# Last attention layer of a four-layer transformer kernel: values as narrow weights, block transposes at a group's end, GpSimd for some shifted copies

## The chip, the cores and the metric

The kernel runs on one core of one Trainium2 chip. Its engines run side by side, each with its own queue of instructions in a fixed order: PE (TensorE, matrix multiplies), DVE (VectorE), ACT (ScalarE), POOL (GpSimd) and SP (SyncE, which issues DMAs). PE writes into PSUM, eight banks of 512 float32 columns by 128 partitions; the others read from there and from SBUF. The metric is the device time of one execution in microseconds (us); the median over runs is compared.

## The reference

An activation `x` of 2048 tokens by 512 channels goes through four layers, each `x = x + f(layernorm(x))`: A, B, A, B. Both have 32 heads of 16 channels.

Layer A cuts the tokens into four segments of 512. Inside a segment it is causal softmax attention; beside it stands a linear-attention memory `M`, `z` that is summed over the earlier segments, and a gate per head mixes the two. Layer B is plain attention over all 2048 tokens:

```
scores = einsum('bhqd,bhkd->bhqk', q, k) * Dh ** (-0.5)
p = softmax(scores)
o = einsum('bhqk,bhkd->bhqd', p, v)
x = x + o.reshape(B, S, D) @ wo
```

All tensors are bfloat16. Nothing subtracts a row maximum in the kernel: it takes exponentials, sums them with a column of ones beside the values, and divides at the end.

## The kernel before, in words

**A planner writes the program.** The class `Sched` (lines 69 to 190) records every operation with its dependencies, and keeps an estimate of the time at which each engine would have done it. `Builder` walks through the work unit by unit, and decides from these estimates what goes next and to which engine. The result is a fixed order of instructions for each engine with semaphore waits between them; on the chip nothing is decided any more.

**Groups and tiles.** Work is cut into groups (`Group`, line 224): one layer, one segment of 512 queries, and four heads (one in each 32-partition quarter `r`). A group of layer B with all four key segments has 64 tiles, a tile being 128 keys by 512 queries of one head. `make_groups` (line 1108) lists them. Layers 0 to 3 overlap in time, since a later layer's segment 0 starts while the earlier layer's last segments run; only the last layer's query segments 1 to 3, 24 groups of 64 tiles, stand alone at the end. Query segment 0 of layers B is done in waves over the key segments, with partial sums kept in SBUF.

**A unit** (`unit`, line 1191) takes two or three tiles for ACT. Their score matmuls (tile `qm,KB`, 32 rows of the array each, four quarters of the rows beside one another) go to banks 0 to 2 or 4 to 6 in turn, ACT takes the exponential of all of them in one instruction (line 1244) into `pT`, and in layers A POOL masks the diagonal blocks (line 1259). Two units later the value products follow.

**Tiles on DVE.** Some tiles of layers B have their exponential made on DVE instead: `dx_find` and `dx_take` (lines 826, 838) take up to a third of a group's tiles, and `compose` (line 1265) puts them beside a unit's tiles. `dx_first` (line 891; the operation is at line 900) reads one or two score banks and turns them with one multiply and add into 16-bit integers whose bits are a bfloat16 near the exponential. `dx_chain` (line 928; line 946) makes three more images of a pair, each by adding a constant. The four images' errors cancel for the most part, so such a tile costs four value products where a tile of ACT costs one. A pair needs four slots of 128x1024 16-bit: nine in `dxw`, and six more in `KA`, `QA`, `VA` once layer 0 no longer needs their second halves (`dx_space`, `dx_widen`, lines 852 and 870). `dx_room` (line 820) lets DVE fall behind by no more than `DQ` = 2200 ns of the estimate. `dx_chain` could give a copy to POOL, but `POOL_ON` is 0.

**The value product** (`pv`, line 1286). The exponentials, 128 keys by 128 queries, are the weights, and the 17 columns of a head's values and ones stream through. A 512-query tile takes four such pairs of weight load and matmul, and its results stand by query in bank 7 (`ACC`), 16 blocks of 17 columns. Products of ACT's tiles are due two units after; products of DVE's images are fitted in by `pv_taken` (line 1364), up to four in a unit, and all that are left when the group ends (`pv_step`, line 1379).

**A group's end** (`finish`, line 1312): a reciprocal of the sums (line 1333) and a product (line 1345) give `ob`, by query. After the second of two groups `run_deferred` (line 1351) sends `ob` through a DMA transpose to `oT`, channels by queries, for the output projection (`task_out`, line 736). The very last group goes through two pairs of PE transposes instead (`last_out`, line 779).

**Beside that** projections, layer norms and output projections are tasks that fill in where the estimates leave room (`bg_one`, line 1013), and `keep_busy` (line 375) issues dummy matmuls (`wB,zero`) where PE's streams would fall under 43% of a window. All recorded matmuls have line 389, or 393 for transposes.

## Time and profile before

| | us |
|---|---|
| three runs | 1953.49, 1959.38, 1965.37 |
| median | 1959.38 |
| the profiled execution | 1956.4 |
| its span, first to last instruction | 1954.7 |
| ACT busy | 1828.6 |
| PE busy | 1761.4 |
| DVE busy | 1500.5 |
| POOL busy | 285.0 |

A row of the groups names line, engine, operation, output and inputs (buffer numbers left out), shapes and count; then busy time in us and the mean of one in ns; then the idle time of the engine just ahead of them, and who ended it. A row of the stretches gives start and end, length, and each engine's busy time with the number of instructions that started, then PE's granted clock as a share, the DMA share and GB/s. A row of the timeline has start, length, engine, line, operation and count; neighbours of one kind are merged into one row. PE is the matmuls, PEld the weight loads.

### The profile page before, as it was taken

Reading aid. Unit: us, or ns where it says so; the run is one execution under the profiler, and the core shown is the slowest. Engines: PE = TensorE matmul, PEld = TensorE weight load, DVE = VectorE, ACT = ScalarE, POOL = GpSimd, SP = SyncE. Lnnn points to the kernel's source line nnn. Section 1 sums busy time; section 2 is a strip of 40 time slices with the busy share of each in tenths; the row PEclk is TensorE's granted clock in tenths of the full one; section 3 lists DMA queues with packets and bytes.
Section 4 is the critical chain, followed back from the end, with each engine's and each line's share of the span. In section 5 each row is a group of like instructions: output and inputs, shape, how many; then the busy total and the mean of one; then the engine's idle time right before and its main releaser. Section 6 shows DMA issues by size and latency. Waiting matters only on the chain.

```text
span 1954.7 us, 79981 instructions
## 1 busy us (share of the span) xinstructions
PE 1761.4 (90%) x35997; PEld 1135.1 (58%) x36232; DVE 1500.5 (77%) x3154; ACT 1828.6 (94%) x1641; POOL 285.0 (15%) x642
## 2 busy tenths in 40 slices
PE   7788888889979999899997999889899999999998
PEld 4344444556646666466664666445666666666665
DVE  5656566788858887688876888577888888888886
ACT  6789988899999999899998999988999999999998
POOL 3432153010050000500005000320100000000000
PEclk9999999999999999899999999999999999999999
DMA  4110111000011000100001001000000000000000
GB/s 152 27 36 18 29 21 31 14 11 11 10 27 16 3 8 14 34 9 14 8 14 37 5 6 24 18 8 13 11 16 9 6 17 6 6 6 16 6 6 16
DMA packets 101016, 35.96 MB, mean 18 GB/s; under 512 B 93505, under 2 KB 100161, under 8 KB 100673
## 3 DMA queue, kind: packets, MB, share of 16 engines
q1 hardware_dynamic: 100672, 30.83, 8.1%
q8 instruction: 283, 4.64, 1.0%
q14 instruction: 61, 0.49, 0.1%
HBM read 6.30 MB, written 2.10 MB: 4 GB/s over the span
## 4 chain that ended last, share of the span: by engine, by line
PE 37%; ACT 36%; DVE 12%; issue 12%; DMA 2%; POOL 1%; SPq 0%; ACTq 0%; DVEq 0%; POOLq 0%
PE ps L389 37%; ACT pT L1244 36%; DVE dxw L900 2%; DVE dxw L946 1%; DMA xT<-xn 1%; DVE ob L1345 1%; POOL pT L1259 1%; ACT amem L584 1%; DVE VA L900 0%; DVE QA L900 0%; DVE rd L1333 0%; DVE QA L946 0%; DVE KA L946 0%; DVE VA L946 0%; DVE KB L416 0%
## 5 line engine op out<-in xcount | busy, mean ns | idle before, releaser
L1244 ACT ACTIVATE pT<-ps 128x1536 bf16<-128x1536 f32 (+3 forms) x1600 | 1799.6, 1260 | 100.6 <-PE ps L389 80.4
L389 PEld LDWEIGHTS ps<-VB,pT 128*128 128x128 bf16 x12872 | 427.9, 96 | 324.6 <-issue 233.3
L389 PE MATMUL ps<-qm,KB 32*128 32x512 bf16 x4096 | 524.4, 387 | 63.2 <-ACT pT L1244 45.8
L389 PE MATMUL ps<-VB,pT 128*128 128x51 bf16 (+1 forms) x12872 | 551.7, 187 | 28.9 <-DVE ob L1345 16.4
L900 DVE TENSOR_SCALAR dxw<-ps 128x512 uint16<-128x512 f32 (+1 forms) x365 | 333.4, 915 | 85.3 <-PE ps L389 80.9
L389 PE MATMUL ps<-VB,dxw 128*128 128x51 bf16 (+1 forms) x8520 | 362.1, 186 | 0.9 <-DVE dxw L946 0.9
L1259 POOL TENSOR_SCALAR_AFFINE_SELECT pT<-pT 128x256 bf16<-128x256 bf16 (+2 forms) x513 | 209.6, 427 | 552.6 <-ACT pT L1244 543.3
L389 PEld LDWEIGHTS ps<-VB,dxw 128*128 128x128 bf16 x8520 | 282.3, 96 | 1.4 <-DVE dxw L946 1.1
L389 PEld LDWEIGHTS ps<-qm,KB 32*128 32x128 bf16 x4096 | 130.0, 91 | 179.0 <-ACT pT L1244 97.7
L1161 POOL TENSOR_SCALAR qm<-QB,par 128x512 bf16<-128x512 bf16 x86 | 68.1, 794 | 1020.2 <-PE ps L389 895.1
L946 DVE TENSOR_SCALAR dxw<-dxw 128x1024 uint16<-128x1024 uint16 (+1 forms) x454 | 182.8, 423 | 3.3 <-PE ps L389 0.7
L389 PE MATMUL ps<-qm,KA 32*128 32x512 bf16 (+3 forms) x1024 | 105.0, 312 | 36.0 <-ACT pT L1244 31.4
L389 PE MATMUL ps<-VA,pT 128*128 128x51 bf16 (+1 forms) x2560 | 114.9, 190 | 22.8 <-DVE ob L1345 14.4
L389 PEld LDWEIGHTS ps<-VA,pT 128*128 128x128 bf16 x2560 | 87.1, 98 | 79.1 <-POOL pT L1259 43.5
L389 PEld LDWEIGHTS ps<-qm,KA 32*128 32x128 bf16 x1024 | 30.0, 92 | 112.5 <-ACT pT L1244 77.8
L900 DVE TENSOR_SCALAR KA<-ps 128x512 uint16<-128x512 f32 (+1 forms) x91 | 80.2, 882 | 18.8 <-PE ps L389 17.6
L389 PE MATMUL ps<-VB,QA 128*128 128x51 bf16 (+1 forms) x1848 | 90.0, 186 | 0.0
L900 DVE TENSOR_SCALAR VA<-ps 128x512 uint16<-128x512 f32 (+1 forms) x83 | 75.2, 906 | 18.7 <-PE ps L389 17.6
L389 PE MATMUL ps<-VB,KA 128*128 128x51 bf16 (+1 forms) x1844 | 89.0, 185 | 0.1
L389 PE MATMUL ps<-VB,VA 128*128 128x51 bf16 (+1 forms) x1836 | 87.3, 185 | 0.0
L900 DVE TENSOR_SCALAR QA<-ps 128x512 uint16<-128x512 f32 (+1 forms) x82 | 74.5, 909 | 14.5 <-PE ps L389 13.8
L1333 DVE RECIPROCAL rd<-ps 128x16 f32<-128x16 f32 x112 | 28.3, 253 | 69.6 <-PE ps L389 69.1
(125 smaller groups left out, 1540.0 us busy)
## 6 DMA issues: line engine op xcount, KB each, us to landing
out_dram<-x SPq DMA_DIRECT2D x8, 256.0 KB, 2.2
x<-in_A_x_dram SPq DMA_DIRECT2D x3, 512.0 KB, 9.0
wB<-in_B_wqkv_dram SPq DMA_DIRECT2D x1, 1536.0 KB, 13.0
oT<-ob SPq DMA_TRANSPOSE x63, 2.4
xT<-xn SPq DMA_TRANSPOSE x60, 2.5
x<-in_A_x_dram SPq DMA_DIRECT2D x4, 128.0 KB, 2.2
wA<-in_A_wk_dram SPq DMA_DIRECT2D x1, 512.0 KB, 4.7
wA<-in_A_wq_dram SPq DMA_DIRECT2D x1, 512.0 KB, 5.7
```

The source lines that it names most:

```text
L389: self.sc.add("pe", lambda e: e.matmul(out, lhsT, rhs, start=start, stop=stop, skip_group_check=True), reads=reads, banks=[(bank, "w", all ...
L584: self.op("act", lambda e: e.activation(et, src, ACT.Exp), reads=bsrc, writes=self.b_amem, ns=1023, gap=915)
L900: self.sc.add("dve", lambda e: e.tensor_scalar(d, o, SCALE * LOG2E * 128, EXP_C, op0=ALU.mult, op1=ALU.add), writes=[w for j in range(k) f ...
L946: self.op(eng, (lambda o, d: lambda e: e.tensor_scalar(o, w, d, None, op0=ALU.add))(o, d), reads=bw, writes=wr, ns=ns, name="dxs")
L1161: self.op(eng, (lambda m, q, col: lambda e: e.tensor_scalar(m, q, col, 0.0, op0=ALU.mult, op1=ALU.add))(m, q, col), reads=[bq, self.b_par] ...
L1244: self.sc.add("act", (lambda dst, src: lambda e: e.activation(dst, src, ACT.Exp, scale=SCALE))(dst, src), writes=self.b_pT[slot * 3 + i:sl ...
L1259: self.op("pool", (lambda blk, pat: lambda e: e.affine_select(blk, blk, pattern=pat, compare_op=ALU.is_ge, fill=0.0, base=0, channel_multi ...
L1333: self.op("dve", lambda e: e.reciprocal(rd, src[:, :, 16]), reads=bsrc, writes=[br], bank=bk, alloc=al, ns=253)
L1345: self.op("dve", lambda e: e.tensor_tensor(ob, src[:, :, 0:16], rb, ALU.mult), reads=[br] + bsrc, writes=[self.b_ob[oi][g.e]], bank=bk, al ...
```

## The change

Six things, most of them for the last layer's groups of 64 tiles (`g.fm`):

1. `pv`: for these groups the 17 columns of values and ones are the weights, and the 512 queries of a tile stream through in one matmul. Its tile of the array is all 128 rows by 32 columns; head `r` uses column quarter `r` and PSUM partitions `32r` to `32r + 16`. The result stands by channel in bank 7, 512 columns.
2. `finish_fm`: at a group's end DVE transposes the bank in 32x32 blocks into `tk` (float32, in the dead half of `KA`), takes the reciprocal of column 16 of each block, multiplies into `of` by query, and after the second group of a pair `run_deferred` transposes `of` in blocks into `oT`. The DMA transposes of these groups go. The last group does this in two halves, in place of the PE transposes.
3. `pv_some` takes the place of `pv_taken`: products due now and shifted products are put in an order in which the column quarter that is free soonest comes first. `pv_close` lets a group's last shifted products wait for a later step, where they were forced at once.
4. POOL may make a shifted copy: `POOL_ON` goes from 0 to 300 and its assumed cost `POOL_T` from 1150 to 1800, so a copy goes to POOL where by the estimate it would be done at most 300 ns after DVE gets there. This holds in layer 1 too, once the first slots have opened. `DQ` goes from 2200 to 3000.
5. `dx_areas`: up to 38 slots in memory that is no longer used (`QA`, `VA`, `wA`, `KA`, `woA`, `phk`, `phq`, keys and values of key slots 2 and 3, `xT`), each opened when the flags that it needs are set, in place of six.
6. The planner's estimate knows column tiles: 30 ns from one to the next, and half a full pass's weight in the activity that `keep_busy` watches.

The two programs in instructions: PE 36232 matmuls before, 28291 after; DVE 3154 and 2811; POOL 638 and 1142; ACT 1640 and 1638; SP 194 and 183.

```diff
             st = max(ready, self.pe_issue())
+            if cols < 128:
+                st = max(st, self.pe_issue() + 30)
...
-            self.streams.append((st, n / 2.4 * rows / 128))
+            self.streams.append((st, n / 2.4 * rows / 128 * max(cols / 128, self.CW)))
...
+        self.fm = kind == "B" and Builder.FM >= (1 if L == 3 and first and last else 2 if L == 3 else 3 if first and last else 4)
...
-    DX_T, POOL_T, POOL_ON = 430, 1150, 0
+    DX_T, POOL_T, POOL_ON = 430, 1800, 300
...
-    DQ, DXS, PVN, PVLATE, PVWAIT = 2200, 4, 4, 600, 0
+    DQ, DXS, PVN, PVLATE, PVWAIT, PVHOLE = 3000, 4, 4, 600, 0, 100
...
+    def dx_areas(self):
...
+        first = (("attn", 0, 3), ("mem", 0, 3))
+        add(flat(self.QA[:, 1, :, :]), 2, lambda j: self.b_QA[1], *first)
+        add(flat(self.VA[:, 1, :, :]), 2, lambda j: self.b_VA[1], *first)
+        add(flat(self.wA[:, :, :]), 6, lambda j: self.b_wA, ("proj", 2, 3))
+        last = (("attn", 2, 3), ("mem", 2, 3), ("op", 2, 3))
+        add(flat(self.KA[:, 0, :, :]), 2, lambda j: self.b_KA[0], *last)
...
+        for ks in (2, 3):
+            add(flat(self.KB[:, ks, :, :]), 2, lambda j: self.b_KB[ks], ("attn", 3, 0))
+            add(flat(self.VB[:, ks, :, :]), 2, lambda j: self.b_VB[ks], ("attn", 3, 0))
+        for k in range(2):
+            add(flat(self.xT[:, k, :, :]), 2, lambda j: self.b_xT[k], ("in", 3, 3))
...
     def dx_widen(self):
 
-        if not self.wide and ("attn", 0, 3) in self.flags and ("mem", 0, 3) in self.flags:
-            self.wide = True
-            self.dx_bufs += range(self.NDX, self.NDX + 6)
+        for n, (_, _, need) in enumerate(self.areas[:self.XDX]):
+            if n not in self.dx_open and all(f in self.flags for f in need):
+                self.dx_open.add(n)
+                self.dx_bufs.append(self.NDX + n)
+                self.wide = True
...
+        if g.fm:
+            g.left -= 1
+            self.mm(self.ps[32 * r:32 * r + 17, bank.col0:bank.col0 + 512], parts[0][2], pT[:, 0:512], r not in g.started, g.left == 0,
+                    [bp, parts[0][3]], bank, g.acc, tile=(128, 0, 32, 32 * r))
+            g.started.add(r)
+            parts = ()
...
+    def finish_fm(self, g, src, bsrc, bk, al):
...
+        for j in range(halves):
+            sl = slice(512 // halves * j, 512 // halves * (j + 1))
+            tk, rd = self.tk[:, sl], self.rd[:, m, n * j:n * j + n]
+            self.op("dve", (lambda tk, a: lambda e: e.transpose(tk, a))(tk, src[:, sl]), reads=bsrc, writes=[self.b_tk] + extra, bank=bk,
+                    alloc=al, ns=690 if halves == 1 else 420)
+            t3 = tk.rearrange("p (n f) -> p n f", f=32)
+            self.op("dve", (lambda rd, t3: lambda e: e.reciprocal(rd, t3[:, :, 16]))(rd, t3), reads=[self.b_tk], writes=[self.b_rd[m]], ns=160)
...
+            self.op("dve", (lambda of, t3, rb: lambda e: e.tensor_tensor(of, t3[:, :, 0:16], rb, ALU.mult))(of, t3, rb),
+                    reads=[self.b_rd[m], self.b_tk], writes=[self.b_of[g.e]], ns=430 if halves == 1 else 300)
...
+            if g.fm:
+                o = self.oT[:, 1, g.c, :]
+                op = self.op("dve", (lambda o: lambda e: e.transpose(o, self.of))(o), reads=self.b_of, writes=[self.b_oT[1][g.c]], ns=690)
...
+    def pv_some(self, g, due, now):
...
+        while True:
+            cand = [(self.pv_quad(e[3]), 0, n) for n, e in enumerate(due)]
+            for n, t in enumerate(self.dxq):
+                if t[1] is g and (now or t[0].end + LAG[t[0].eng] <= self.sc.t["pe"] + self.PVWAIT):
+                    cand.append((self.pv_quad(t[3]), 1, n))
+            if not cand:
+                return
+            q, kind, n = min(cand)
...
+            if not due and not now and q + self.PVHOLE > max(self.pv_quad(r) for r in range(4)) and (
+                    used >= self.PVN or self.sc.t["pe"] > self.sc.t["act"] - self.PVLATE):
+                return
...
+    def pv_close(self, g, must):
...
+        if not whole():
+            self.pv_some(g, (), must)
...
+            if not whole():
+                return 0
+        self.cur = self.pend = None
+        cost = self.finish(g)
```

## The prediction

> **What bounds the kernel now.** I read the page's top first, then the busy time by stretches, cut where the last stretch is the one that the change touches most: from 1421 us on only the last layer's 24 groups of 64 tiles are left (query segments 1 to 3).
>
> ```profile
> span 1954.7 us, 79981 instructions
> PE 1761.4 (90%) x35997; PEld 1135.1 (58%) x36232; DVE 1500.5 (77%) x3154; ACT 1828.6 (94%) x1641; POOL 285.0 (15%) x642
> ```
> ```profile
> core 0: us, PE busy (x) PEld busy (x) DVE busy (x) ACT busy (x) POOL busy (x), PEclk, DMA share, GB/s
> 0.00:442.00 442.00, 371.42 (x5728) 207.22 (x5795) 288.56 (x692) 381.92 (x359) 128.31 (x309) 0.97 0.17 37
> 442.00:1167.00 725.00, 660.81 (x13710) 433.95 (x13804) 574.35 (x1251) 686.89 (x626) 96.72 (x218) 0.98 0.08 14
> 1167.00:1421.00 254.00, 225.22 (x4368) 138.86 (x4406) 188.96 (x407) 235.61 (x209) 44.94 (x95) 0.99 0.08 15
> 1421.00:1949.00 528.00, 502.52 (x12198) 354.49 (x12225) 447.09 (x804) 522.70 (x448) 14.98 (x20) 0.99 0.05 9
> 1949.00:1954.70 5.70, 1.38 (x9) 0.59 (x8) 1.58 (x3) 1.47 (x3) 0.00 (x0) 1.00 0.27 92
> ```
> In the last long stretch ACT is busy 522.7 of 528 us. PE has 502.5, which looks as full, but DVE has 447.1 and POOL 15. Only one of ACT and PE can set the pace, so I went to the groups of that stretch, each with its idle time and what ended it.
>
> ```profile
> L1244 ACT ACTIVATE pT<-ps 128x1536 bf16<-128x1536 f32 x257 | 396.9, 1619 | 1.9 <-PE ps L389 1.5
> L1244 ACT ACTIVATE pT<-ps 128x1024 bf16<-128x1024 f32 x191 | 227.9, 1194 | 1.8 <-PE ps L389 1.5
> L389 PEld LDWEIGHTS ps<-qm,KB 32*128 32x128 bf16 x1518 | 44.9, 91 | 61.3 <-ACT pT L1244 36.3
> L1161 POOL TENSOR_SCALAR qm<-QB,par 128x512 bf16<-128x512 bf16 x20 | 15.0, 749 | 426.1 <-PE ps L389 403.9 <-DVE dxw L900 22.2
> L900 DVE TENSOR_SCALAR dxw<-ps 128x1024 uint16<-128x1024 f32 x106 | 129.4, 1220 | 31.0 <-PE ps L389 29.2
> L900 DVE TENSOR_SCALAR dxw<-ps 128x512 uint16<-128x512 f32 x8 | 5.5, 690 | 2.2 <-PE ps L389 2.1
> L946 DVE TENSOR_SCALAR dxw<-dxw 128x1024 uint16<-128x1024 uint16 x184 | 74.4, 429 | 1.6
> L1333 DVE RECIPROCAL rd<-ps 128x16 f32<-128x16 f32 x24 | 6.2, 257 | 21.9 <-PE ps L389 21.5
> L1345 DVE TENSOR_TENSOR ob<-ps,rd 128x256 bf16<-128x256 f32 x24 | 10.2, 424 | 0.8
> ```
> ACT's exponentials wait 3.7 us in 528; PE's score matmuls wait 36 us for ACT. So **ACT sets the pace here**, with PE close behind. One 512-column tile more costs ACT 1619 - 1194 = 425 ns. In the earlier stretches no engine is that full (ACT 95% and PE 91% from 442 to 1167 us), and an ACT saving there counts in part.
>
> **The change, part by part.** Counts are of the two programs in the order in which each engine is given them.
>
> *Tiles moved off ACT.* In the last stretch ACT gets 1153 score tiles now and 1100 after; DVE's first passes take 420 in place of 368. The number of exponentials stays (448, 447). 53 x 0.425 = **-22.5 us** where ACT sets the pace. Before that stretch ACT's tiles go +2, +17 and -12: +7 tiles, +3.0 us at most; I take half, +1.5. PE's products there change by -252 and +168 small ones of 31 ns (the load rows below), -8 and +5 us, so PE gives nothing worth a line.
>
> *The value product.* Now a tile costs four 128x128 weight loads with 34 or 51 columns each. After, in the last stretch, it is one load of 17 columns and one 512-column pass that fills a quarter of the array's columns: 2820 passes take the place of 10644 products. The trace has no matmul of that shape. Its nearest rows:
>
> ```profile
> 1599.82 0.38 PE L389 MATMUL ps<-woB,oT 128*128 128x512 bf16 x1
> ...
> 1601.80 0.55 PEld L389 LDWEIGHTS ps<-woB,oT 128*128 128x128 bf16 x4 [0.23 <-DVE dxw L900]
> 1601.80 1.04 PE L389 MATMUL ps<-woB,oT 128*128 128x512 bf16 x4
> ...
> 1608.15 0.10 PEld L389 LDWEIGHTS ps<-qm,KB 32*128 32x128 bf16 x3
> 1608.16 0.39 PE L389 MATMUL ps<-qm,KB 32*128 32x512 bf16 x3
> ...
> 1610.67 0.37 PEld L389 LDWEIGHTS ps<-VB,pT 128*128 128x128 bf16 x12 [0.23 <-issue]
> ```
> Four full-array passes of 512 columns take 1.04 us, and one alone 0.38, so they start (1.04 - 0.38)/3 = 0.22 apart. Three quarter-array passes in different *rows* take 0.39 us together, as one does: quarters run side by side. Small products come 0.37/12 = 31 ns apart: 10644 x 0.031 = 330 us now. After: if quarter *columns* run side by side as quarter rows do, the price is that of the longest chain on one quarter; walking the new order, the 448 runs of passes hold 902 such links, 902 x 0.22 = 198 us. If they don't, 2820 x 0.22 = 620 us. I take 198, because the row tiles are the nearest shape. The score matmuls keep their 447 x 0.33 = 148 us (0.10 of loads and the 0.23 idle for "issue"), other matmuls 74 x 0.22 = 16. PE then needs 362 of some 510 us. The relief itself buys nothing: PE was not the bound. It only lets 53 tiles move without PE becoming it, since a moved tile costs four products.
> The Trainium skill, "TensorE: Matmul & The Clock Gate", section "Part 3: Packing small matmuls", gives 2.38x for three column tiles of 32 columns; by that figure the estimate would be 2820 x 0.22 / 2.38 = 261 us, still no bound.
>
> *DVE and the group's end.* Copies of line 946 on DVE go from 553 to 364 in the stretch, because POOL makes 275 (pairs, 128x1024). Their price and that of the first pass, whole stretch:
>
> ```profile
> 1421.00:1949.00 528.00, 208.31 (x553) 0.99 0.05 9
> ...
> 1421.00:1949.00 528.00, 225.57 (x191) 0.99 0.05 9
> ```
> These are DVE's busy times by source line, line 946 first, then line 900. 208.3/553 = 0.377 us: -189 x 0.377 = -71 us. First passes: 2 more pairs x 1.22 and 48 more singles x 0.69 = +36 us. A group's end was a reciprocal and a product (0.26 + 0.42); now a 32x32 transpose out of PSUM stands ahead of them, and one more for every second group. No transpose of this kind is in the trace; bounds are 0.26 (the short reciprocal) and 1.22 (two banks read); I take the 0.69 of one bank read. 23 x (0.69 + 0.35) = +24 us. DVE: 447 - 71 + 36 + 24 = **436 us**. 11 DMA transposes leave SP's queue, which was no bound: nothing. The next group's first product waits for the transpose as it now waits for the product of line 1345: 0.69 against 0.68. The last group's halved transposes take the place of two PE transposes and their copies: +0.5 us.
>
> *POOL's copies.* POOL has no copy of this kind now. One row gives 0.69 us for 512 columns; twice that is 1.38, and the lone row's slope can't be under zero: 0.69 to 1.38, and I take 1.15 (masks on POOL go from 308 ns at 128 columns to 539 at 384, 0.9 ns a column, so 0.69 + 0.46).
>
> ```profile
> L1259 POOL TENSOR_SCALAR_AFFINE_SELECT pT<-pT 128x384 bf16<-128x384 bf16 x126 | 67.9, 539 | 439.2 <-ACT pT L1244 438.9
> L1259 POOL TENSOR_SCALAR_AFFINE_SELECT pT<-pT 128x128 bf16<-128x128 bf16 x128 | 39.4, 308 | 89.0 <-ACT pT L1244 88.6
> ```
> 275 x 1.15 = 316 us of 510: POOL has room. Its copies are read some ten units later, so being late costs nothing; the unused memory (up to 38 slots more) is what allows that lead and has no price of its own. Behind them on POOL's queue stand the masked query copies (line 1161), which now idle 426 us ahead of 15 us of work: a group's lead is left for them. But POOL and DVE get in each other's way:
>
> ```profile
> 1504.72 0.42 DVE L946 TENSOR_SCALAR dxw<-KA 128x1024 uint16<-128x1024 uint16 x1
> 1505.22 1.23 DVE L900 TENSOR_SCALAR dxw<-ps 128x1024 uint16<-128x1024 f32 x1
> 1505.31 0.69 POOL L1161 TENSOR_SCALAR qm<-QB,par 128x512 bf16<-128x512 bf16 x1 [20.52 <-PE ps L389]
> ...
> 1592.25 1.05 POOL L1161 TENSOR_SCALAR qm<-QB,par 128x512 bf16<-128x512 bf16 x1 [21.24 <-PE ps L389]
> 1592.40 0.42 DVE L946 TENSOR_SCALAR dxw<-KA 128x1024 uint16<-128x1024 uint16 x1
> 1592.74 0.84 DVE L946 TENSOR_SCALAR KA<-KA 128x1024 uint16<-128x1024 uint16 x1
> ```
> Beside a first pass (read from PSUM) POOL's 0.69 and DVE's 1.23 stay what they are. Beside a copy (SBUF to SBUF) POOL's own time grows to 1.05 and a copy that arrives during it goes from 0.42 to 0.84. So an instruction of 512 columns holds DVE's copies off for 0.42 us, one of 1024 for 0.85. Bounds for the stretch: nothing, if each falls beside a first pass; 275 x 0.85 = 234 us, if each stops a copy for its whole length. Between, by chance meetings: POOL holds 234 of 510 us (46%), half a hold is left on average, 364 x 0.46 x 0.42 = 70 us. I take that, since first passes fill most of DVE's time: DVE 436 + 70 = **506 us**. Behind a stopped copy on DVE stand first passes, whose PSUM banks the score matmuls of the unit after next need; that is the way by which a late DVE reaches ACT.
> The Trainium skill, "SBUF — State Buffer", section "SBUF: two separate sides", calls the port pair that the two share an exclusive lock, held for the full instruction while the loser blocks. The trace agrees on who blocks, and its 0.42 of a 0.69 us instruction is less than the full length.
>
> *The sum.* ACT after: 528 - 22.5 = 505.5 us; DVE 506. Two engines that are level wait for one another here and there, and DVE's first passes still wait for scores (31 us in the row above), so I take 510: **-18 us**. Earlier stretches +1.5, the end +0.5: -16. The profiled execution took 1956.4 us (span 1954.7), so 1940; the three runs shown have their median at 1959.4, 3 above it: **1943 us**.
>
> **Rivals.**
> *Slower: POOL and DVE exclude each other so often that DVE becomes the bound.* For it: after the forecast's own meetings DVE is already level with ACT. Against: copies are 137 of DVE's 436 us, and nothing else of it was seen to be stopped. If every second POOL copy costs a full hold, 275 x 0.5 x 0.85 = 117, DVE needs 553 us, +25 on 528; with +2 of the other parts 1956.4 + 27 + 3 = 1986. It eats the gain from 0.25 us lost per POOL copy (506 against 436) and loses time from 0.34 (528). The skill's section just named, with the hold as long as the instruction, speaks for this case.
> *No change to be seen.* The same loss between 0.25 and 0.34 us per copy, or POOL's 216 copies and 6 short ones ahead of the last stretch delaying the masks there (POOL is the one engine that makes both) and giving back as much as ACT saves: 1950 to 1968, say 1958.
> *Column tiles don't run side by side.* PE then needs 620 + 148 + 16 = 784 us, +256: about 2215. It decides once a pass costs over (510 - 164)/2820 = 0.12 us, fewer than 1.8 at a time. The row tiles' 0.39 us for three speaks against it.
> *Better than forecast.* POOL always falls beside first passes, and PE's and DVE's lighter load shortens the middle stretch by a per cent: 1930.
> The softer group end, which no longer forces shifted products in, can't be the surprise:
>
> ```profile
> L389 PE MATMUL ps<-VB,dxw 128*128 128x51 bf16 (+1 forms) x8520 | 362.1, 186 | 0.9 <-DVE dxw L946 0.9
> ```
> PE waited 0.9 us for copies in the whole execution.
> That the change doesn't do what it says can only mean here that the tiles don't leave ACT; the order is fixed when the program is built, so it isn't one.
>
> **How the numbers follow.** Forecast 0.52 (1936 to 1949); no change 0.21 (1958); POOL against DVE 0.15 (1986); columns one by one 0.05; better 0.07 (1930). The range leaves out the columns' case, the upper part of the port's and a sliver below: 1930 to 1985. Half a per cent, about what a measurement of this kernel can tell from no change, is 9.8 us: under 1949.6 is faster. That gives faster 0.58, same 0.22, slower 0.20.
>
> **What would show it.** In the stretch of the 24 groups: ACT still waits under 10 us, and its 1536- and 1024-column exponentials number about 207 and 239; the new 17-row passes come in fours with about 0.4 us for the four; DVE copies have a mean between 0.45 and 0.65 us where it was 0.43; POOL's take 1.1 to 1.6 us each; PE is idle over a quarter of the time. If ACT's idle time ended by PE is above 20 us with PE in turn waiting for DVE, the port rival holds; if PE is full, the columns rival. I would be wrong also if the stretch from 442 to 1167 us moved by more than 8 us either way.

## The result and the profile after

The changed kernel takes **2386.5 us** (median of 4 runs, 2379.3 to 2394.0) beside 1960.5 for the kernel before: 1.217 times as long, 95% interval 1.214 to 1.220. The forecast was 1943.

The top of the page of the changed kernel, with the granted clock and POOL in 40 slices and the chain that ended last by engine:

```profile
span 2383.7 us, 64939 instructions
...
PE 1943.9 (82%) x28291; PEld 938.3 (39%) x28291; DVE 1629.3 (68%) x2811; ACT 1843.2 (77%) x1639; POOL 1677.0 (70%) x1146
...
POOL 4502456593536646588626566999999999999997
PEclk9999999989898898989999899777777877777778
...
POOL 32%; PE 11%; issue 7%; DVE 6%; ACT 4%; POOLq 0%; ACTq 0%; DVEq 0%
```
POOL went from 285 us of work to 1677 and leads the chain. From the 26th slice on, a little ahead of the last 24 groups, it is full. The same four stretches as in the prediction, cut at the same groups' ends (columns as there: PE, PEld, DVE, ACT, POOL, then the clock):

```profile
0.00:461.00 461.00, 388.57 (x5827) 212.30 (x5828) 296.03 (x669) 384.97 (x360) 210.23 (x337) 0.96 0.16 36
461.00:1265.00 804.00, 716.32 (x13506) 449.08 (x13503) 572.71 (x1058) 695.95 (x624) 461.78 (x352) 0.90 0.07 13
1265.00:1559.00 294.00, 250.36 (x4559) 152.36 (x4556) 206.71 (x378) 234.40 (x208) 215.10 (x161) 0.91 0.06 13
1559.00:2379.00 820.00, 588.06 (x4412) 124.41 (x4409) 551.99 (x706) 526.70 (x447) 789.91 (x297) 0.77 0.01 3
```
442, 725, 254 and 528 us have become 461, 804, 294 and 820: +19, +79, +40 and +292. In the last stretch POOL is busy 790 of 820 us; ACT, which was busy 522.7 of 528, now stands still for over a third of the time (293 of 820 us). POOL's and DVE's copies (line 970) in that stretch:

```profile
1559.00:2379.00 820.00, 773.64 (x275) 0.77 0.01 3
...
1559.00:2379.00 820.00, 260.63 (x363) 0.77 0.01 3
```
The first row is POOL: 773.64/275 = **2.81 us** a copy. 275 of them are more than the 528 us that the stretch had. The second is DVE: 0.72 us a copy, where it was 0.377. ACT's groups in the stretch show that the tiles did leave ACT (207 and 239 exponentials, where it was 257 and 191). The rows behind them show who waits for whom now, with the total in us, the number of waits and the longest:

```profile
L1268 ACT ACTIVATE pT<-ps 128x1536 bf16<-128x1536 f32 x207 | 299.3, 1454 | 157.8 <-PE ps L398 156.7
L1268 ACT ACTIVATE pT<-ps 128x1024 bf16<-128x1024 f32 x239 | 243.5, 1026 | 133.2 <-PE ps L398 131.3
```
```profile
ACT pT L1268 <- PE ps L398: 288.0, 215, 10.7
...
PEld ps L398 <- POOL dxw L970: 49.1, 29, 4.0
...
PEld ps L398 <- POOL KB L970: 34.7, 18, 10.2
...
PE ps L398 <- POOL KB L970: 27.0, 17, 9.9
```
ACT waits for PE's scores (288 us, 215 times), and PE stands in front of passes whose image POOL has not made yet, up to 10 us at a time; all such waits of PE's weight loads together are 254 us. PE's queue is in a fixed order, so the scores behind such a pass wait too.

A piece of the time line shows two points that the forecast left open, columns side by side and what POOL keeps from DVE:

```profile
1800.59 3.01 POOL L970 TENSOR_SCALAR KB<-VB 128x1024 uint16<-128x1024 uint16 x1
1800.79 1.25 DVE L970 TENSOR_SCALAR QA<-VB 128x1024 uint16<-128x1024 uint16 x1
...
1801.21 0.39 PE L398 MATMUL ps<-pT,VB 128*17 128x512 bf16 x3
...
1801.22 0.59 PE L398 MATMUL ps<-wA,VB 128*17 128x512 bf16 x2
...
1801.43 0.38 PE L398 MATMUL ps<-woA,VB 128*17 128x512 bf16 x1
1801.44 0.38 PE L398 MATMUL ps<-VB 128*17 128x512 bf16 x1
...
1801.96 0.41 DVE L970 TENSOR_SCALAR dxw<-wA 128x1024 uint16<-128x1024 uint16 x1
```
Seven column passes are done in 0.61 us (1801.21 to 1801.82); four start within 0.02 us, and the next ones 0.21 later. So quarters in columns do run side by side. And beside one POOL copy, a DVE copy that starts 0.2 us into it takes 1.25 us, while one that starts 1.37 us into it takes its usual 0.41.

### The profile page after: what moved, and what is told of

The parts are those of the page before. It is cut to its first block, busy times and chain, and to the rows that moved or that the text cites. A ratio compares the mean times of both kernels' runs of the same rounds, so it can differ in the third digit from the quotient of the medians.

```text
span 2383.7 us, 64939 instructions
## 1 busy us (share of the span) xinstructions
PE 1943.9 (82%) x28291; PEld 938.3 (39%) x28291; DVE 1629.3 (68%) x2811; ACT 1843.2 (77%) x1639; POOL 1677.0 (70%) x1146
## 4 chain that ended last, share of the span: by engine, by line
POOL 32%; PE 11%; issue 7%; DVE 6%; ACT 4%; POOLq 0%; ACTq 0%; DVEq 0%
PE ps L398 11%; POOL dxw L970 8%; POOL wA L970 5%; ACT pT L1268 4%; POOL VA L970 4%; POOL KB L970 3%; POOL QA L970 3%; POOL xT L970 2%; POOL woA L970 2%; POOL VB L970 1%; POOL phq L970 1%; POOL KA L970 1%; DVE dxw L924 1%; POOL phk L970 1%; DVE dxw L970 1%
## 5 line engine op out<-in xcount | busy, mean ns | idle before, releaser
L398 PE MATMUL ps<-qm,KB 32*128 32x512 bf16 x4096 | 597.7, 433 | 54.9 <-ACT pT L1268 26.4
L398 PE MATMUL ps<-VB,pT 128*128 128x51 bf16 (+1 forms) x8256 | 366.2, 190 | 36.0 <-DVE ob L1378 14.5
L398 PEld LDWEIGHTS ps<-VB,pT 128*128 128x128 bf16 x8256 | 289.6, 98 | 244.7 <-issue 151.2
L970 POOL TENSOR_SCALAR dxw<-dxw 128x1024 uint16<-128x1024 uint16 x98 | 278.9, 2847 | 96.9 <-DVE dxw L924 79.8
L398 PE MATMUL ps<-VB,dxw 128*128 128x51 bf16 (+1 forms) x5148 | 225.9, 189 | 30.5 <-POOL dxw L970 29.8
L398 PE MATMUL ps<-pT,VB 128*17 128x512 bf16 x1108 | 215.6, 466 | 15.8 <-DVE KA L1396 15.6
L398 PEld LDWEIGHTS ps<-VB,dxw 128*128 128x128 bf16 x5148 | 178.3, 99 | 36.2 <-POOL dxw L970 33.7
L398 PE MATMUL ps<-dxw,VB 128*17 128x512 bf16 x362 | 121.5, 478 | 37.6 <-POOL dxw L970 37.0
L398 PE MATMUL ps<-qm,KA 32*128 32x128 bf16 (+3 forms) x1024 | 105.6, 317 | 35.8 <-ACT pT L1268 33.1
L970 POOL TENSOR_SCALAR dxw<-VA 128x1024 uint16<-128x1024 uint16 (+1 forms) x33 | 89.0, 2697 | 35.9 <-DVE VA L924 29.6
L398 PE MATMUL ps<-wA,VB 128*17 128x512 bf16 x238 | 91.1, 469 | 26.5 <-POOL wA L970 25.7
```

Of the source, the lines that this page charges most:

```text
L398: self.sc.add("pe", lambda e: e.matmul(out, lhsT, rhs, start=start, stop=stop, skip_group_check=True), reads=reads, banks=[(bank, "w", all ...
L970: self.op(eng, (lambda o, d: lambda e: e.tensor_scalar(o, w, d, None, op0=ALU.add))(o, d), reads=bw, writes=wr, ns=ns, name="dxs")
```

## The experiments

Theory P: POOL's copies are the loss, as a queue that is too long and as time in which DVE's copies are kept out. Its rivals: the column product and the low clock (C), the new order with its soft group end (S). The table has the lengths of the four stretches, cut at the same groups' ends, and the count of POOL copies in each (by the programs' order; by the traces up to five more or fewer). Code below is shortened.

| kernel | us | stretches, us | POOL copies | us each in the last |
|---|---|---|---|---|
| before | 1955 to 1961 | 442, 725, 254, 528 | 0 | |
| after | 2386.5 | 461, 804, 294, 820 | 30, 129, 63, 275 | 2.81 |
| e1 no POOL copies | 1958.6 | 446, 725, 253, 522 | 0 | |
| e2 before, with POOL copies | 2059.4 | 459, 779, 279, 534 | 31, 108, 57, 14 | |
| e3 planner knows 2.85 us | 2108.7 | 454, 771, 269, 608 | 16, 86, 36, 176 | 2.85 |
| e4 old value product | 2340.5 | 463, 808, 294, 773 | 30, 129, 63, 257 | 2.82 |
| e5 int32 copies | 2074.2 | 456, 743, 271, 597 | as after | 1.12 |
| e6 bf16 copies | 2388.4 | 462, 802, 294, 817 | as after | 2.81 |
| e7 idle POOL copies | 2072.1 | 445, 733, 262, 625 | 150 extra, 144 of them in the last | 2.86 |
| e8 columns everywhere, no POOL | 1943.1 | 448, 713, 255, 528 | 0 | |
| e10 e8 with more filling matmuls | 1976.6 | 456, 723, 262, 534 | 0 | |
| e11 copies of 8 columns | 1988.4 | 454, 732, 268, 523 | as after | 0.39 |
| e12 multiply and add | 1995.6 | 451, 735, 267, 537 | as after | 1.30 |
| e13 the same, last stretch only | 1977.0 | 446, 729, 256, 544 | 0, 0, 0, 273 | 1.29 |
| e14 the same, price known | 2027.4 | 448, 744, 269, 557 | 36, 168, 80, 362 | 1.24 |
| e15 e8 and e13 together | 1989.0 | 443, 709, 253, 573 | 0, 0, 0, 369 | 1.22 |

**e1: POOL makes no copies.** `POOL_ON = 300` becomes `POOL_ON = 0`; all the rest of the change stays. The planner then gives out another order.

> The changed kernel with every shifted copy back on DVE (POOL_ON = 0); column product, 32x32 transposes and extra slots stay. In the last 24 groups DVE then makes some 594 copies and ACT 1127 tiles. Theory P (POOL is the bound: 275 copies of 2.85 us are 784 of the last stretch's 820 us, and before that masks stand behind copies): all of the loss goes. Last stretch 528 - 26 x 0.425 = 517 us, DVE 447 + 15 (copies) + 17 (first passes) + 24 (group ends) = 503 of it; whole 1940 to 1960, clock back to about 0.99. Rival C (the column product makes the array slow: granted clock 0.77 in the last stretch, 433 ns a score matmul): the clock stays near 0.77 and the time stays over 2150. Rival S (the softer group end and the new order): the stretch from 442 us on stays 60 us or more longer than before, whole over 2020.

1958.6 us, 1.0027 of before (1.0002 to 1.0052). The last stretch's row:

```profile
1424.00:1946.00 522.00, 441.19 (x4330) 116.10 (x4353) 486.75 (x924) 513.82 (x450) 17.98 (x20) 1.00 0.02 5
```
Theory P holds, C and S fall: the clock is back at 1.00 with the column product in place, so the 0.77 came with POOL's copies and not with the column product. PE was busy 588 of 820 us at 0.77 and is busy 441 of 522 here; that its standing still brought the clock down is likely, but no run shows it by itself. The whole loss goes when POOL makes no copies. The row also shows what the rest of the change is worth together: nothing to speak of. PE's weight loads fall from 354 to 116 us, but ACT stays the bound with 514 of 522.

**e2: the kernel before, with POOL copies**, in before.py:

```
-    DX_T, POOL_T, POOL_ON = 430, 1150, 0
+    DX_T, POOL_T, POOL_ON = 430, 1800, 300
```


> The kernel before with POOL allowed to make copies by the change's own rule (POOL_ON = 300, POOL_T = 1800), nothing else of the change. Its planner gives POOL some 31 copies up to 442 us, 108 and 54 in the two middle stretches and only 14 in the last, since it has only six slots more. Theory P: the middle loses what it lost in the changed kernel (about 19 + 98 + 40 us), the last stretch stays within 15 us of 528; whole 2060 to 2130. Rival S (the middle's loss comes from the new order and the soft group end): 1955 to 1970.

2059.4 us, 1.054 of before. Its second and last stretch:

```profile
459.00:1238.00 779.00, 687.96 (x13501) 444.44 (x13602) 582.64 (x1081) 692.92 (x622) 404.14 (x329) 0.93 0.08 13
...
1517.00:2051.00 534.00, 503.46 (x12227) 354.64 (x12255) 451.02 (x796) 525.83 (x450) 55.13 (x36) 1.00 0.04 9
```
This is at the lower edge of what P expected: with POOL's copies alone the earlier stretches lose 17, 54 and 25 us (P had 98 for the second), and the last, with 14 copies, 6. One reason that P gave was wrong: PE's weight loads wait 23 to 24 us for masks in the second and third stretch of before, e1, e12 and the changed kernel alike. POOL's masks do not suffer; in the changed kernel's two stretches PE's weight loads wait 54 us, and its matmuls 48, for the copies themselves.

**e3: the planner knows the price.** `POOL_T = 2850` in the changed kernel.

> The changed kernel whose planner is told what a POOL copy takes (POOL_T 2850 in place of 1800). It then gives POOL 176 copies in the last 24 groups and not 275, and ACT 1122 tiles. Theory P: 176 x 2.85 + 15 = 517 us of POOL in a stretch of 515 to 560 us; the whole 1945 to 2050, the middle still 30 to 90 us longer than before because masks stand behind copies. Rival C (clock and columns): the last stretch stays over 700 us.

2108.7 us, outside of what P expected. The last stretch:

```profile
1494.00:2102.00 608.00, 501.78 (x4343) 121.44 (x4359) 565.00 (x758) 526.72 (x450) 514.84 (x196) 0.91 0.01 4
```
POOL does have its 515 us and is not full (85%); now **DVE** is the fullest, with 565 of 608. Its copies (line 970) in e1's last stretch, and in e3's:

```profile
1424.00:1946.00 522.00, 218.34 (x599) 1.00 0.02 5
...
1494.00:2102.00 608.00, 296.03 (x433) 0.91 0.01 4
```
At e1's 218.34/599 = 0.365 the 433 copies would take 158 us; they take 296. So 138 us are lost on DVE beside 174 POOL copies, 0.79 us for each, while a copy on DVE costs 0.365. A POOL copy takes more from DVE than it saves, here.

**e4: the old value product** in all groups but the last two:

```
-        self.fm = kind == "B" and Builder.FM >= (...)
+        self.fm = (kind, L, qseg, c) == ("B", 3, 3, 3)
```


> The changed kernel with the old value product in all groups but the last two; POOL makes 257 copies in the last 24 groups, ACT 1072 tiles. Theory P: 257 x 2.85 + 15 = 747 us of POOL; last stretch 750 to 800, whole 2300 to 2370, as slow as with the column product. Rival C: without the column passes the last stretch comes back under 560 us and the whole under 2130, with the clock at 0.99.

2340.5 us: nearly as slow without the column product, as P says, and the clock is low here too. Its last row has POOL at 740 of 773:

```profile
1565.00:2338.00 773.00, 608.06 (x12498) 406.75 (x12512) 591.33 (x756) 514.50 (x443) 740.44 (x279) 0.83 0.03 6
```

**e5: the same bits as int32**, **e6: the same copy as bf16.** Why does a copy take 2.8 us, when line 1185 (1161 in the kernel before) takes 0.69 for half the columns? The order of instructions is the changed kernel's in both.

```
+k32 = bcast(self.kd[:, 2 * j:2 * j + 2].bitcast(dt.int32), [[0, n // 2]])
+tensor_tensor(o.bitcast(dt.int32), w.bitcast(dt.int32), k32, ALU.add)      # e5, on POOL
+tensor_scalar(o.bitcast(bfloat16), w.bitcast(bfloat16), d, None, op0=ALU.add)  # e6, on POOL
```


> The changed kernel in the same order of instructions; POOL's copies add the shift to pairs of values as one int32 (a tensor and a constant column, 512 numbers of 4 bytes in place of 1024 of 2), the same bits as before. Theory P (POOL pays by the number): half the numbers, so 0.7 to 1.5 us a copy, POOL at most 275 x 1.5 + 15 = 428 us of the last stretch and no longer the bound. What then bounds is DVE with the time POOL keeps it out: 552 us in the changed kernel if each copy still costs DVE 0.47 us, 424 + 70 = 494 if half of that; last stretch 510 to 600, whole 1945 to 2070. Rival B (POOL pays by the byte): 2.77 us a copy or more as before, whole 2380 or above.

> The changed kernel in the same order of instructions; only the type changes in which POOL reads and writes its copies: bf16 in place of uint16, so the shift is added to the value and not to its bits and the output is another one. Theory P (the type sets POOL's price: line 1185 makes 512 bf16 columns in 0.69 us, a uint16 copy of 512 columns took 1.49): 1.35 to 1.4 us a copy, POOL 275 x 1.38 + 15 = 395 us of the last stretch; DVE is the bound with 0.3 to 0.5 us lost per POOL copy, 424 + 82 to 138; last stretch 520 to 590, whole 1960 to 2080. Rival B (1024 columns cost POOL 2.77 us whatever the type): 2380.

e6 takes 2388.4 us, as the changed kernel does, and its copies as long as before:

```profile
L971 POOL TENSOR_SCALAR dxw<-dxw 128x1024 bf16<-128x1024 bf16 x98 | 279.5, 2854 | 96.6 <-DVE dxw L924 78.4 <-DVE lnw L516 7.6 <-PE ps L398 5.5
```
The type is not what makes it slow; P's reason for the price fell. e5 takes 2074.2 us with copies of 1.12 us:

```profile
1470.00:2067.00 597.00, 503.82 (x4409) 118.76 (x4409) 539.17 (x704) 514.74 (x447) 320.58 (x293) 0.91 0.01 4
```
Here POOL has 321 us of work, nearly what the forecast gave it (316), and the stretch still takes 597. DVE is busy 539; its copies:

```profile
1470.00:2067.00 597.00, 249.63 (x363) 0.91 0.01 4
```
249.63 - 363 x 0.365 = 117 us are lost there, 0.43 for each POOL copy. No engine is full; the rest must be waits between PE, ACT and DVE, which no run takes apart. So the length of POOL's queue was one loss, and a second stands behind it.

**e7: copies that nobody waits for.** e1 with 150 more copies on POOL, meant for the last stretch, from a weight to dead memory:

```
+if ("attn", 3, 0) in self.flags:
+    self.extra += 1
+    if self.extra % 4:
+        self.sc.add("pool", tensor_scalar(self.spare[0], wB..., 22.0, None, op0=ALU.add), ns=0, gap=0)
```


> The changed kernel with all copies on DVE (as in e1_no_pool) and 150 more copies of 1024 uint16 columns on POOL in the last 24 groups, from a weight into memory that nobody reads: extra work whose result nobody waits for. POOL holds 150 x 2.77 + 18 = 434 of some 520 us. Theory L (a POOL copy keeps DVE's copies out; the run with POOL's true cost shows 0.79 us lost on DVE per POOL copy): DVE 487 + 150 x 0.5 to 0.8 = 562 to 607 us, last stretch 570 to 625 in place of 522, whole 2005 to 2060. Rival Q (only the wait for late copies costs time): last stretch 520 to 530, whole 1950 to 1965.

2072.1 us, and 0.75 us lost on DVE for each of the 144 that fall into the stretch (595.01 - 486.75 over 144; the other 6 run just ahead of it):

```profile
1440.00:2065.00 625.00, 515.74 (x4343) 126.80 (x4343) 595.01 (x920) 527.33 (x449) 428.18 (x164) 0.93 0.01 4
```
That is the second loss by itself: POOL's work costs 100 us though no instruction depends on it.

**e9: eight forms of the operation on POOL**, 25 times each, beside e1's work (a single run, 2087.3 us):

```
0 tensor_scalar(v, u, 22.0, None, op0=add)          uint16, 1024
1 tensor_scalar(v, u, col, None, op0=add)
2 tensor_scalar(v, u, 22.0, 0.0, op0=add, op1=add)
3 tensor_scalar(v, u, col, 0.0, op0=add, op1=add)
4 as 0, 512 columns
5 tensor_scalar(c, a, col, 0.0, op0=mult, op1=add)  bf16, 512: the form of line 1185
6 as 5, 1024 columns
7 tensor_scalar(c, a, col, None, op0=mult)          bf16, 1024
```


> As e7_idle_copies (all copies on DVE, extra work on POOL that nobody waits for), but the 198 extra operations of the last 24 groups take eight forms in turn: uint16 1024 columns add of a constant (the change's copy); the same with the addend in a column; with a second operation (+ 0.0) and constants; with a column and the second operation; 512 columns of the first; bf16 512 columns times a column + 0.0 (line 1185's own form); 1024 columns of that; and 1024 columns times a column without the second operation. Theory O (one operation in place of two takes another, slower path): the five forms without the second operation 2.8 us (1.5 at 512), the others 1.4 (0.69 at 512). Theory I (a constant in the instruction is what is slow, a column quick): forms 1, 3 and 5 slow, the rest 1.35 to 1.4. Theory M (adding is slow, multiplying quick): forms 1 to 5 slow, 6 to 8 quick. Theory W (the number of columns): all forms of 1024 columns 2.8. In each, DVE's copies that start within one last up to 1.25 us, and the last stretch stays 40 to 110 us longer than the 522 us without extra work.

(The expectation counts from 1; without a second operation are its forms 1, 2, 5 and 8, four and not five.) The groups, mean ns behind the comma; lines 976 to 983 are the forms in their order:

```profile
L979 POOL TENSOR_SCALAR wA<-wB,par 128x1024 uint16<-128x1024 uint16 x25 | 98.0, 3918 | 2.2
L978 POOL TENSOR_SCALAR wA<-wB 128x1024 uint16<-128x1024 uint16 x25 | 93.3, 3734 | 2.2
L983 POOL TENSOR_SCALAR wA<-wB,par 128x1024 bf16<-128x1024 bf16 x25 | 77.1, 3083 | 2.3
L977 POOL TENSOR_SCALAR wA<-wB,par 128x1024 uint16<-128x1024 uint16 x25 | 75.4, 3017 | 2.1
L976 POOL TENSOR_SCALAR wA<-wB 128x1024 uint16<-128x1024 uint16 x25 | 71.4, 2855 | 2.2
L980 POOL TENSOR_SCALAR wA<-wB 128x512 uint16<-128x512 uint16 x25 | 41.4, 1656 | 2.2
L982 POOL TENSOR_SCALAR wA<-wB,par 128x1024 bf16<-128x1024 bf16 x25 | 31.2, 1247 | 2.2
L981 POOL TENSOR_SCALAR wA<-wB,par 128x512 bf16<-128x512 bf16 x25 | 18.7, 747 | 2.2
```
None of the four theories has it whole. **Multiply-then-add is one quick form**: 1.25 us here for 1024 columns, 1.12 in the shortest. Every other form of 1024 columns takes 2.9 us and up, the multiply without an add (3.1) and the add with a second add (3.7) too. Line 1185, on which the forecast priced the copy, is of the quick form.

**e12: the copy in the quick form**, with the same result: times a column of ones, plus the shift.

```
+self.op(eng, tensor_scalar(o, w, self.one[:, 0:1], d, op0=ALU.mult, op1=ALU.add))   # on POOL
```
**e11: copies of 8 columns**, to see what the order itself costs.

```
+m = n if eng == "dve" else 8
+self.op(eng, tensor_scalar(o[:, 0:m], w[:, 0:m], d, None, op0=ALU.add))
```


> The changed kernel in nearly the same order of instructions, but each of POOL's copies shifts only the first 8 of its 1024 columns; the rest of the slot keeps what it held (memory is set to one value ahead of its first use), so the sum lacks most of what POOL adds. All waits, all matmuls, DVE's share and the column product stay. Theory P+L (the whole loss is the length of POOL's copies, as a queue and as time in which DVE's copies are kept out): the forecast's other steps then hold, ACT 528 - 53 x 0.425 = 505.5 us and DVE about 436 in the last stretch, which takes 505 to 520; the middle 720 to 735; whole 1925 to 1950 and the clock 0.97 or more. Rival R (the order with the soft group end, the column product or the low clock cost by themselves): last stretch over 530, whole over 1965.

> The changed kernel in the same order, POOL's copies written as times a column of ones plus the shift, in place of plus the shift alone: the same result in uint16. Theory F (multiply and add is the one quick form, 1.12 us at 1024 columns in e9_pool_forms): 1.1 to 1.3 us a copy, the price that the forecast took, POOL 330 us of the last stretch; what is left is what a copy keeps from DVE, 0.37 to 0.42 us each: DVE 535 to 545 as in e5_int32_copy, last stretch 580 to 605, whole 2050 to 2085. Rival T (the quick form is one of bf16 only): 2.8 us or more a copy, whole 2370 to 2700. Rival 1 (the price of 1.15 was the only thing wrong in the forecast): whole 1940 to 1960.

e12 takes 1995.6 us, 1.020 of before (1.016 to 1.023): 391 us less than the changed kernel, in the same order of instructions. e5, with copies as short but 0.43 us kept from DVE for each, was 312 us less, so the length of the copies is by far the larger part. e12 is better than theory F expected (2050 to 2085): this form keeps DVE out for less. DVE's 363 copies in the last stretch take 189.67 us, 57 over 132, so 0.21 for each POOL copy. Rival T falls (uint16 is as quick), and so does rival 1: with nearly the price that the forecast assumed the kernel is still slower than before. The last three stretches, and DVE's copies in the last:

```profile
451.00:1186.00 735.00, 675.24 (x13526) 428.87 (x13523) 539.02 (x1058) 691.35 (x624) 253.44 (x352) 0.97 0.08 14
1186.00:1453.00 267.00, 239.21 (x4543) 146.14 (x4539) 201.31 (x377) 231.91 (x208) 124.02 (x164) 0.96 0.07 14
1453.00:1990.00 537.00, 464.82 (x4409) 115.26 (x4409) 475.89 (x706) 507.31 (x448) 369.38 (x294) 0.97 0.02 4
...
1453.00:1990.00 537.00, 189.67 (x363) 0.97 0.02 4
```
e11, with POOL nearly empty, takes 1988.4 us, so theory P+L failed for the whole (1925 to 1950), and rival R's whole (over 1965) is right. The last stretch is between the two, 523 where P+L had 505 to 520 and R over 530:

```profile
454.00:1186.00 732.00, 681.40 (x13546) 431.01 (x13542) 509.98 (x1061) 690.73 (x624) 137.08 (x352) 0.96 0.08 14
1186.00:1454.00 268.00, 239.43 (x4532) 145.46 (x4530) 188.87 (x378) 231.69 (x208) 89.67 (x188) 0.95 0.07 14
1454.00:1977.00 523.00, 455.09 (x4418) 111.97 (x4417) 433.25 (x713) 505.04 (x449) 124.43 (x299) 0.96 0.02 5
```
The three stretches ahead of it take 1454 us where e1 takes 1424 and before 1421.

**e13: quick copies in the last stretch alone.** The condition `self.wide` becomes `("attn", 3, 0) in self.flags`; **e14: quick copies with their price known**, `POOL_T = 1250` in e12; **e15**: e13 with that price and the column product in all groups (`FM = 4`).

> e12_mult_add (quick form) with POOL copies in the last 24 groups alone, 273 of them; ahead of those the order is that of e1_no_pool. Theory M (in the earlier stretches POOL copies cost by themselves: 9 + 10 + 13 us in e12_mult_add, and much the same with copies of 8 columns): the earlier stretches come back to 446, 725 and 253 us; the last stays 530 to 540; whole 1955 to 1968. Rival O (the order with the column product and the soft group end is what costs there): they stay 25 us or more longer, whole 1980 to 2000.

> e12_mult_add with the planner told the quick form's price (POOL_T 1250): 204 POOL copies in the second and third stretch minus 12 more early ones than before, 362 in the last, where ACT keeps 1079 tiles. Theory H (DVE loses 0.2 us per quick copy, planner's order otherwise right): last stretch 528 - 74 x 0.425 = 497 us of ACT, POOL 362 x 1.25 = 453, DVE under 470; last stretch 505 to 535; earlier stretches as in e12_mult_add or 5 to 10 longer; whole 1975 to 2005. Rival: with the price known the middle comes back too, whole under 1960.

> Everything the runs so far speak for: column product in all groups of the second kind (as e8_all_columns, 1943), POOL copies in the quick form, at its price of 1250 ns and only in the last 24 groups (369 copies, ACT 1087 tiles in place of 1129). Theory H: ACT 528 - 66 x 0.425 = 500 us in the last stretch, POOL 461, which takes 505 to 530; the earlier ones 448, 713 and 255 as in e8_all_columns; whole 1920 to 1950. Rival (what ACT saves is lost to waits between four nearly full engines): 1945 to 1970.

e13 takes 1977.0 us, where 1955 to 1968 was expected: ahead of the last stretch it is back at 446, 729 and 256, so M holds there and O falls. Giving POOL copies *there*, with the order that comes with it, costs some 22 us (1453 to 1431), with copies of 8 columns as with quick ones. Its last stretch takes 544, more than expected:

```profile
1431.00:1975.00 544.00, 470.99 (x4419) 113.88 (x4419) 479.76 (x704) 509.40 (x449) 368.70 (x294) 0.95 0.02 4
```
e14 takes 2027.4, outside of what was expected: with the price known the planner gives POOL 87 more copies in the last stretch (362), ACT is down to 502 us of work, and the stretch is 20 us longer. e15 takes 1989.0, which is the rival's side and beyond:

```profile
1405.00:1978.00 573.00, 489.26 (x4467) 117.42 (x4461) 499.44 (x662) 506.40 (x449) 467.55 (x390) 0.92 0.01 4
```
Four engines between 468 and 506 of 573 us wait for one another; ACT waits 60 us for PE. With quick copies every step that moved more copies to POOL made the last stretch longer: 522 (none), 537 to 544 (273 to 275), 557 to 573 (362 to 369).

**e8: the column product in every group of the second kind, no POOL copies** (`POOL_ON = 0`, `FM = 4`), and **e10**, the same with more filling matmuls (`CW = 0.25`).

> The changed kernel with all copies on DVE and the column product in every group of the second kind, not the last layer's alone (FM = 4): matmuls up to the last stretch fall from 23800 to 11680. Theory M (PE, at 91 to 93% in the middle, sets part of the pace there): the three earlier stretches shrink by 10 to 30 us in all, whole 1925 to 1950. Rival A (ACT alone sets the pace, 95% there): 1950 to 1965 as without it. Rival G (longer group ends on DVE, 0.7 + 0.35 us each, and a transpose ahead of the next group's products): 1965 to 1985.

> e8_all_columns (column product in all groups of the second kind, all copies on DVE) with column passes weighed at a quarter, not half, of a full pass where the planner decides on filling matmuls (CW = 0.25): 340 more matmuls, ACT 1473 and 1125 tiles in the second and last stretch in place of 1484 and 1129. Theory K (the clock, 0.966 in e8_all_columns and 0.984 without the column product in the middle, still costs there): clock 0.975 or more, whole 1932 to 1942. Rival N (the clock costs nothing where ACT sets the pace): 1940 to 1948.

e8 takes **1943.1 us, 0.993 of before (0.990 to 0.996)**, 0.7% faster than the kernel before. The time is theory M's (1925 to 1950). The second stretch is 713 us where it is 725 in e1, with PE busy 631 in place of 656; the three earlier stretches together are 8 us shorter than e1's here, just under M's 10 to 30, and 19 in e15, which has the same order up to there:

```profile
448.00:1161.00 713.00, 631.42 (x5981) 194.50 (x5977) 583.77 (x1268) 678.22 (x635) 96.61 (x222) 0.96 0.06 11
```
e10 takes 1976.6 us; both K and N missed it. The clock hardly moved (0.969), and 340 more matmuls with a somewhat other order cost 33 us. They have no one place: every stretch is longer than in e8, by 8, 10, 7 and 6 us. Why is open.

## Why the prediction was wrong

- **ACT sets the pace, 53 tiles are worth 22.5 us of ACT.** The tiles left as counted; the saving was smaller, and little of it reached the end. The forecast's 505.5 is a length, 528 - 22.5; ACT's busy time, 522.7, would be 500.2 by the same step, and e11 has 505.0. That is 17.7 us, 0.33 a tile in place of 0.425. Even there the stretch takes 523, 5 us less than before, since ACT waits 13.5 us for PE where it was 2.9. A tile fewer on ACT is a tile more with four passes, a first pass and three copies; that ACT waits for these is likely and not shown.
- **Columns side by side.** Right; the time line shows it.
- **DVE's own work, 436.** Right: 433.3 in e11. The 32x32 transpose, taken at 0.69 us, measured 0.71 (line 1396).
- **The group's end, 0.69 against 0.68 for PE.** It was put at nothing, and it was not nothing. In the last stretch of the kernel before, PE's weight loads waited 4.5 us for line 1345; for the transposes they wait 16.8 us in e1 and 26.4 in e12. In e1 the stretch is none the longer (522). In e12 ACT waits 24.5 us for PE, and the stretch takes 537 us with ACT busy 507 and DVE 476, where the sum had 4 us for waits; how much of that is the group's end, no run shows.
- **"275 x 1.15 = 316 us of 510: POOL has room."** The step that failed. A copy takes 2.81 us, so 774 of what should have been 510. Both ends of the bound (0.69 to 1.38) came from a row of another form: line 1161 of the kernel before (1185 after) multiplies and adds, where the copy only adds, and e9 and e12 show that of the forms tried only multiply-then-add is quick. In that form the guess of 1.15 was good (1.12 to 1.30). The step's error is worth the most: e12 wins back 391 of the 426 us, its copies also keeping DVE out for less, and e5, which keeps DVE out nearly as long as the changed kernel, 312.
- **"So being late costs nothing."** It holds as long as POOL has room. With POOL full, lateness adds up until PE waits in order for a copy, up to 10 us, and ACT behind it. No rival had POOL itself as the bound. The point from which it decides could have been worked out from the prediction's own numbers: (510 - 15)/275 = 1.80 us a copy, and the planner's own `POOL_T` in the diff is 1800 ns.
- **What POOL keeps from DVE.** Taken at 70 us for 275 copies, 0.25 each. With copies as they are: 0.47 (changed kernel), 0.75 (e7), 0.79 (e3); in the quick form 0.21, near what was taken. The rival that had this at 0.43 was of the right kind, but it had DVE as the bound and not POOL. A DVE copy costs 0.365, so POOL relieves DVE only where it takes less than that from it; of the forms tried, that is the quick one.
- **Earlier stretches +1.5.** +138 in the changed kernel, where the second stretch alone moved by 79 us and the forecast named 8 as a sign of being wrong; in the quick form still +32 (1453 against 1421). e2 and e13 show that this comes with POOL's copies there. Why copies of 8 columns cost as much as quick ones is open: PE hardly waits for POOL's copies there (0.2 us in e11), and its waits for masks are about as before; the clock is 0.95 to 0.97 in place of 0.97 to 0.99, and e11 also sets memory on POOL there. That order with all copies on DVE was not tried, so the order itself may be the cause.

The forecast's time equals that of e8 by chance: a kernel without POOL's copies.

## What to carry to other kernels

A price is taken from a row of the same operation, not only of the same engine and size; where no such row exists, the bound has no upper end, and the question is at which price the engine becomes the bound and whether anything excludes it. Work moved to an idle engine is worth what it saves on the full one, less what the two take from each other: here a copy given to POOL saved DVE 0.365 us and cost it up to 0.79. An engine with 500 idle microseconds was worth nothing as a second copier, in any form that was tried.

## What the hardware showed that was not expected

Of the forms of POOL's tensor-by-scalar operation that e9 has, one is quick, multiply then add: 1.12 us for 1024 columns of 16 bits; the add alone takes 2.77, the add and add 3.64, the multiply alone 2.85 (shortest of 25 each, uint16 or bf16 as in e9's forms).

A POOL copy does not keep DVE's copies out for its whole length. Time lines of the changed kernel, POOL's and DVE's:

```profile
1898.14 2.81 POOL L970 TENSOR_SCALAR xT<-QA 128x1024 uint16<-128x1024 uint16 x1
1901.02 2.82 POOL L970 TENSOR_SCALAR QA<-wA 128x1024 uint16<-128x1024 uint16 x1
...
1899.99 1.23 DVE L970 TENSOR_SCALAR dxw<-wA 128x1024 uint16<-128x1024 uint16 x1
1901.14 1.25 DVE L970 TENSOR_SCALAR VA<-dxw 128x1024 uint16<-128x1024 uint16 x1
```
A copy that starts 0.12 us or 1.85 us into a POOL copy takes 1.25 us or nearly so. Those that started 0.9 to 1.58 us into one took 0.41 or 0.42, all 111 that the time line of the changed kernel's last stretch shows singly. So there are two stretches of about 0.84 us (1.25 - 0.41) in each POOL copy that adds alone, with about a microsecond free between them. The Trainium skill, "SBUF — State Buffer", section "SBUF: two separate sides", has the pair of ports locked for the whole instruction; these rows do not agree with that.

The same program takes longer in the runs with a lower granted clock: e1's ten runs go from 1953.2 us at 0.984 to 1970.9 at 0.966, about 1 us for 0.001.
